# A gated linear attention and a maxout feed-forward block on one core: the written step order, the PSUM rooms and the set of second-engine steps are exchanged for others

## The chip, the cores and the metric

The kernel runs on one core of a Trainium2 chip. The metric is the device time of one execution in microseconds; the time of a kernel is the median of several executions. Five engines of the core work side by side, each on its own list of instructions: TensorE (PE, with its weight loads shown as PEld), VectorE (DVE), ScalarE (ACT), GpSimd (POOL) and SyncE (SP). The last two mainly issue transfers here. Every matmul and every DMA has float32 data; the weights come in memory as 64-bit floats.

## The reference

The attention part keeps, per head, a complex state that each step multiplies by a gate and to which it adds the outer product of k and v; the output is q times the state's real part. The feed-forward part takes the largest of three projections and projects it down.

```python
mag = np.sqrt(a_re * a_re + a_im * a_im)
scale = np.minimum(mag, 0.999) / (mag + 1e-06)
a_re_n, a_im_n = (a_re * scale, a_im * scale)
...
for t in range(S):
    ar, ai = (a_re_n[:, :, t, :, None], a_im_n[:, :, t, :, None])
    new_re = ar * S_re - ai * S_im
    new_im = ar * S_im + ai * S_re
    kv = np.einsum('bhd,bhe->bhde', k[:, :, t], v[:, :, t])
    S_re, S_im = (new_re + kv, new_im)
    y[:, :, t] = np.einsum('bhd,bhde->bhe', q[:, :, t], S_re)
...
h = np.maximum(np.maximum(x @ w1, x @ w2), x @ w3)
return (h @ w_out).astype(np.float32)
```

Here q, k, v, a_re and a_im are 4 batches × 8 heads × 768 tokens × 48; x is 3072 × 384, w1 to w3 are 384 × 768 and w_out is 768 × 384.

## The kernel before, in words

The 3072 tokens are worked in 12 groups, g = 0 to 11. A group is one chunk of 128 tokens of two batches, which the names tell apart by an x or a y. Two batches run through their six chunks, then the other two.

Nothing is left to a scheduler. The string SCHEDULE (line 21) lists 1903 words, each a step and the group that it is for (`dky:0` is step dk of the second sequence of group 0), and `program` (998) runs them in this order through `run` (954). The class Bound (199) ties each engine's instructions to the one before it on that engine, so the string is the order on every engine, and also the order in which SP and POOL issue DMAs. Steps on different engines wait for one another only where data or a buffer demand it. A DMA that waits on SP holds up all DMAs behind it in SP's list.

Every output of TensorE goes to one of four PSUM rooms. `banks` (218) takes the next digit of the string SLOTS (124) as the room. So a step on TensorE waits until the steps that read the room's last contents are done.

The set OTHER (131) names the words that run on their second engine. `copy` (239) is on ScalarE, or on VectorE if the word is in the set; `magnitude` (246) likewise; `increase` (253) is an accumulating DMA issued by POOL, or an addition on VectorE; the loads of q, k and v (379, 385) are issued by SP, or by POOL if in the set. ScalarE needs a table load whenever the next function is of another set, exponential and logarithm on the one side, sine and arctangent on the other (`activation`, 227).

The steps that matter here, by their words:

- Loads: Lr, Li are a_re and a_im of a group (192 KB, tiles ar and ai), Lq, Lk, Lv are q, k, v in four DMAs of 48 KB each (tiles q, k, vb). WL0 to WL11 (`weight_load`, 414) bring a third of a weight matrix each as raw 64-bit words, 768 KB, always on SP, into a borrowed buffer: xhx, strassen or a part of another weight's place (dictionary ROOMS, 138). WL4 and WL7 both use strassen, WL2, WL5 and WL8 use xhx, so a load waits for the last conversion step of the one before.
- Conversion of the raw words to float32 (`weight_step`, 429): Wa on ScalarE, Wb, Wc, We, Wf on VectorE; Wf is the last that reads the raw words. Wg adds w1's negative to w2 or w3, by `increase`: a 384 KB accumulating DMA `w<-w` unless in OTHER.
- Gates of a group (names in line 499): sqr, sqi, add, lnL, expw, expe, lne, relu, Lnop, abs, addw, lnw, half, expL, mulai, mulw, stt, atan, xor, turn. They turn ar and ai into a log magnitude Ln and an angle w; `turn` is the angle's last step. In group 0 they run in two halves, named by 0 and 1.
- cs: TensorE's running sum of the angles; t and nf reduce it to one turn, af, sa and sb make cosine and sine. sums, En, Ek, Eq: running sums of Ln and their exponentials. F, f0 to f3: a few cut-off factors.
- mk, mq, uk, uq: k and q times exponentials and sines, on VectorE. tpk, tpq: transposes on TensorE; Kc, Qc: their copies; Q1, Q2, KB, QB, QG: further scaled copies.
- A, B: score matmuls (64 and 32 small ones). g0 to g3, b0, b1: masks and copies into atm. dk, h0 to h3: state update. y: the output, 128 × 384; x: its copy to SBUF (xT in group 0, part of xhx later).
- T, t, M, m: the product w1·w_out, needed because the kernel takes the maximum over x(w2−w1), x(w3−w1) and 0, and brings w1's part in behind it as x(w1·w_out).
- U, u: up-projection and maximum (U01, U11 and so on: half and weight; group 0 in thirds with x or y, as `U01x:0`). S, P, r, O, o: down-projection, from group 1 on by seven products. D: store. J: joins of weights for the seven products. Cd: four tiny accumulating DMAs of POOL that carry the angle to the next chunk. CL, Z: constants and zeros.

In the order before, VectorE's neighbourhood of the change reads uqy:0, turn:1, mky:0, Wf4:0; SP's reads Lqx:1, WL5, WL7, WL8, Lix:4; TensorE's reads M2:0, csx:1, tpky:0, Fx:1, csy:1, Ay:0, U01x:0, dky:0, U11x:0. Every instruction is recorded through one helper, so all profile rows carry line 208 and are told apart by tile names.

Of the kernel before, what the change touches and what calls it, by code (L numbers as in the profile page):

```python
# [21 lines left out]
Liy:0 sqi1:0 Zg:0 Zf:0 Lry:0 sqr1:0 Lix:0 add1:0 lnL1:0 sqi0:0 Lrx:0 sqr0:0 add0:0 expw1:0 WL0:0 WL3:0 expe1:0 relu1:0  # L22
lne1:0 lnL0:0 xor0:0 Wa0:0 expe0:0 expw0:0 Lnop1:0 xor1:0 abs1:0 lne0:0 half1:0 Wb0:0 Wc0:0 We0:0 Fy:0 pw1:0 f0y:0
relu0:0 WL6:0 Lqx:0 Lnop0:0 Wa3:0 abs0:0 WL10:0 WL9:0 Lix:1 Wf0:0 lnw1:0 sumsx:0 Wa6:0 Wb3:0 half0:0 Wc3:0 Lkx:0 Eqx:0
Wb6:0 f1y:0 expL1:0 We3:0 mulw1:0 pw0:0 Ekx:0 Lrx:1 Liy:1 f3y:0 Wc6:0 lnw0:0 Wf3:0 Lry:1 Fx:0 mulai1:0 expL0:0 mulw0:0
mulai0:0 stt1:0 stt0:0 Enx:0 We6:0 f3x:0 atan0:0 turn0:0 T0:0 atan1:0 t0:0 mkx:0 Wa9:0 Wf6:0 csx:0 turn1:0 Wb9:0 tx:0
mqx:0 Wa10:0 nfx:0 WL11:0 afx:0 csy:0 Wb10:0 ty:0 sqr:1 Wc9:0 Wc10:0 T2:0 nfy:0 sbx:0 sax:0 We9:0 ukx:0 Wf9:0 f1x:0
t2:0 f2x:0 We10:0 Lix:2 uqx:0 Lky:0 f2y:0 tpkx:0 kEnx:0 Wf10:0 f0x:0 sqi:1 Wa11:0 WL1:0 Wb11:0 add:1 sumsy:0 Eky:0
tpqx:0 CL:0 Qcx:0 Kcx:0 Wa1:0 Q2x:0 lnL:1 WL2:0 Q1x:0 Eqy:0 relu:1 Wb1:0 Wc11:0 T1:0 expe:1 Eny:0 Wc1:0 expw:1 abs:1
Lvx:0 Lry:2 t1:0 We11:0 dkx:0 h1x:0 xor:1 Ax:0 Wf11:0 Wa2:0 Lqy:0 lne:1 g0x:0 We1:0 Liy:2 g1x:0 Lkx:1 Wb2:0 QBx:0  # L30
# [7 lines left out]
u02x:0 atan:2 U12y:0 turn:2 sbx:1 Wf7:0 u01y:0 u02y:0 Lix:4 u11y:0 Fy:1 Wg7:0 sumsy:1 Wa8:0 Wb8:0 mkx:1 u12y:0 mqx:1  # L38
U21y:0 sby:1 f0y:1 Wc8:0 csx:2 Lnop:2 f1y:1 f3y:1 Lkx:2 f2y:1 Z4:0 Eky:1 csy:2 Eny:1 u21y:0 Eqy:1 uqx:1 ty:2 tpqx:1
Qcx:1 U21x:0 We8:0 ukx:1 tpkx:1 u21x:0 Lvx:2 Wf8:0 nfy:2 Kcx:1 tx:2 Z3:0 Wg8:0 Lky:1 kEnx:1 sumsx:2 nfx:2 Fx:2 U22y:0  # L40
h0x:1 u22y:0 Lvx:1 QBx:1 say:1 Lqy:2 dkx:1 Liy:3 mqy:1 Q1x:1 Enx:2 Q2x:1 mky:1 afx:2 sax:2 Lvy:2 KBx:1 h1x:1 sbx:2
# [5 lines left out]
lne:3 QBx:2 kEnx:2 lnw:3 Lry:4 U11:1 h3y:1 g1x:2 Cdy:2 g2x:2 u11:1 uqy:2 expL:3 mulai:3 U12:1 g3x:2 u12:1 tpqy:2 Qcy:2
tpky:2 dkx:2 Fy:2 Lnop:3 mulw:3 U01:1 f0y:2 Lqy:3 stt:3 h0x:2 h1x:2 h2x:2 J1:0 f3y:2 sqi:4 Kcy:2 U02:1 f2y:2 sqr:4
h3x:2 atan:3 Lix:5 f1y:2 add:4 Liy:5 J2:0 KBx:2 u01:1 Cdx:2 turn:3 Bx:2 kEny:2 b1x:2 b0x:2 csx:3 tx:3 csy:3 lnL:4
h0y:2 ty:3 KBy:2 u02:1 Fx:3 expe:4 f2x:3 nfx:3 S1:1 nfy:3 f3x:3 S3:1 dky:2 sumsx:3 Q1y:2 h1y:2 Q2y:2 f1x:3 Ekx:3 f0x:3  # L50
Lkx:3 Enx:3 afy:3 QBy:2 Lky:4 h2y:2 S2:1 P1:1 P5:1 S4:1 yx:2 Eqx:3 J4:0 Ay:2 g0y:2 Lrx:5 xx:2 mkx:3 relu:4 Py:1 afx:3
P4:1 h3y:2 expw:4 r1:1 abs:4 addw:4 g1y:2 g2y:2 lne:4 P6:1 xor:4 sax:3 QGy:2 g3y:2 Px:1 sby:3 P7:1 sbx:3 Dx:0 P3:1
mqx:3 r6:1 half:4 h0x:3 P2:1 By:2 r5:1 r7:1 r57:1 oy:1 lnw:4 sumsy:3 b1y:2 b0y:2 Fy:3 ukx:3 Cdx:3 Eny:3 uqx:3 Eky:3
expL:4 ox:1 Cdy:3 Eqy:3 f3y:3 Lvy:3 f0y:3 yy:2 xy:2 tpqx:3 mulai:4 tpkx:3 Qcx:3 mqy:3 Lnop:4 mulw:4 QBx:3 Q1x:3 Lky:3
say:3 stt:4 sqi:5 uqy:3 Lry:5 sqr:5 Kcx:3 KBx:3 mky:3 U01:2 Lvx:3 Q2x:3 U02:2 f2y:3 uky:3 add:5 f1y:3 Dx:1 u01:2 u02:2
tpqy:3 Lqx:4 tpky:3 atan:4 Kcy:3 Ax:3 lnL:5 S3:2 Qcy:3 Liy:6 Bx:3 g0x:3 g1x:3 g2x:3 kEnx:3 Lkx:4 U11:2 turn:4 g3x:3
xor:5 csy:4 QGx:3 Lqy:4 b0x:3 u11:2 b1x:3 csx:4 ty:4 tx:4 nfx:4 afx:4 nfy:4 Q2y:3 dkx:3 sumsy:4 Eqy:4 sumsx:4 Ekx:4
mkx:4 h1x:3 mqy:4 expe:5 kEny:3 Eqx:4 Q1y:3 KBy:3 U12:2 Eky:4 h2x:3 Enx:4 yx:3 expw:5 Eny:4 Ay:3 u12:2 sax:4 P7:2
sbx:4 h3x:3 S1:2 Lry:6 QBy:3 g0y:3 g1y:3 S2:2 P1:2 sby:4 mqx:4 Fx:4 h0y:3 relu:5 Dy:1 xx:3 g2y:3 g3y:3 dky:3 abs:5
Fy:4 QGy:3 h1y:3 h2y:3 h3y:3 r1:2 afy:4 say:4 f0y:4 uqx:4 f2y:4 f3y:4 P5:2 addw:5 P6:2 Py:2 lnw:5 expL:5 uqy:4 ukx:4  # L60
r6:2 f2x:4 lne:5 Lnop:5 Lrx:6 f1y:4 Px:2 S4:2 P2:2 r5:2 P4:2 By:3 h0y:4 Lqx:5 half:5 Cdy:4 f3x:4 r7:2 b0y:3 Lkx:5
Cdx:4 r57:2 mulai:5 f0x:4 mky:4 uky:4 b1y:3 P3:2 ox:2 oy:2 f1x:4 mulw:5 stt:5 yy:3 xy:3 tpqy:4 Qcy:4 Q2y:4 atan:5
turn:5 tpqx:4 Qcx:4 QBx:4 Q1x:4 Q2x:4 Lix:7 tpky:4 Q1y:4 tpkx:4 Lix:6 sqr:6 sqi:6 U11:3 U12:3 u11:3 Kcy:4 add:6 kEnx:4
Kcx:4 csy:5 u12:3 lnL:6 csx:5 expe:6 kEny:4 Ax:4 ty:5 nfy:5 lne:6 xor:6 Ay:4 tx:5 nfx:5 relu:6 expw:6 g0x:4 abs:6 Dy:2
Lvx:4 g1x:4 g2x:4 g3x:4 U01:3 g0y:4 g1y:4 afx:5 Lqy:5 sax:5 g2y:4 u01:3 g3y:4 sbx:5 S3:3 U02:3 h0x:4 KBx:4 QGx:4 dkx:4
u02:3 sumsx:5 half:6 Lvy:4 addw:6 afy:5 lnw:6 expL:6 h1x:4 Lnop:6 h2x:4 h3x:4 S1:3 Dx:2 sumsy:5 dky:4 Lrx:7 Lky:5
Liy:7 Eqx:5 Eqy:5 Eny:5 P1:3 sby:5 mqx:5 h1y:4 P7:3 Eky:5 S2:3 mqy:5 P5:3 Bx:4 Lry:7 mulai:6 b0x:4 P6:3 mky:5 h2y:4
uqx:5 KBy:4 b1x:4 QBy:4 h3y:4 mulw:6 Enx:5 S4:3 yx:4 Ekx:5 sqr:7 By:4 r1:3 r6:3 xx:4 stt:6 Fx:5 r5:3 r7:3 Lvx:5 QGy:4
mkx:5 r57:3 b0y:4 f3x:5 say:5 atan:6 Py:3 Px:3 P3:3 P2:3 turn:6 f0x:5 b1y:4 uqy:5 P4:3 sqi:7 Lqy:6 f2x:5 f1x:5 csx:6
ukx:5 tx:6 csy:6 ty:6 ox:3 yy:4 oy:3 nfy:6 uky:5 xy:4 tpqx:5 nfx:6 Dx:3 sby:6 tpkx:5 add:7 Lvy:5 Qcx:5 Q1x:5 kEnx:5  # L70
Q2x:5 Kcx:5 tpky:5 tpqy:5 Kcy:5 U11:4 u11:4 Fy:5 kEny:5 dkx:5 sbx:6 Qcy:5 Lvy:6 afy:6 xor:7 lnL:7 Lvx:6 f2y:5 f3y:5
f1y:5 h0x:5 f0y:5 Q2y:5 h1x:5 sumsy:6 Lry:8 expw:7 afx:6 Ax:5 g0x:5 Eny:6 relu:7 g1x:5 g2x:5 expe:7 h0y:5 Lky:6 Liy:8
Eqy:6 Q1y:5 abs:7 U01:4 u01:4 sax:6 QGx:5 half:7 Cdx:6 mqy:6 g3x:5 U12:4 say:6 Eky:6 KBx:5 QBx:5 addw:7 lnw:7 mky:6
U02:4 Lrx:8 expL:7 u12:4 Bx:5 uqy:6 Ay:5 b1x:5 mulai:7 lne:7 u02:4 S3:4 Lqx:7 sumsx:6 g0y:5 dky:5 b0x:5 h1y:5 KBy:5
P1:4 P7:4 Enx:6 g1y:5 Eqx:6 Lqx:6 yx:5 QBy:5 Ekx:6 g2y:5 g3y:5 By:5 xx:5 S1:4 mqx:6 tpqy:6 uqx:6 mulw:7 tpqx:6 b0y:5
Dy:3 Qcy:6 P5:4 S2:4 P6:4 b1y:5 stt:7 Px:4 P2:4 Py:4 P4:4 Lnop:7 QGy:5 Lix:8 S4:4 atan:7 r1:4 r6:4 r5:4 r7:4 sqr:8
# [965 lines left out]
```

## Time and profile before

| what | value |
|---|---|
| time, median of 3 runs | 568.42 us (568.22 to 568.48) |
| the profiled execution's own time | 566.42 us |
| its span, from the first to the last instruction | 564.7 us |
| mean granted TensorE clock | 0.978 |
| bytes moved | 47.53 MB, mean 84 GB/s |
| of these HBM | read 33.03 MB, written 4.72 MB |

The profiled execution is 2.0 us below the median of the runs, and 1.7 us lie outside its span. Times in the rows are in microseconds from the span's start. Where the page divides the span into 40 equal slices of 14.1 us, the busy tenths of two engines and the granted clock are:

```
PE   2568799999998999999999999999999999999997
DVE  7999959999998999999999889999998868997324
PEclk9779989999999999999999999999999999999999
```

Each digit is one slice. TensorE is filled from the sixth slice on, and the granted clock is below full speed in a few slices of the first hundred microseconds only. A busy share is an average over such stages, so each stage is looked at by itself.

### The profile page before, as it was taken

What the parts mean: (1) busy time and instruction counts of PE and PEld (TensorE: products, weight loads), DVE (VectorE), ACT (ScalarE), POOL (GpSimd) and SP (SyncE); (2) the same over time, 40 slices, a digit from 0 to 9 for tenths busy, and PEclk for the clock granted to TensorE, in tenths of its full rate; (3) what the DMA queues carried; (4) which work ended last, traced back from release to release, by engine and by line L of the source; (5) the groups of instructions that cost most, each with busy time, mean ns of one, the idle gap of its engine ahead of it and who ended that gap; (6) DMA issues with size and microseconds to landing.
All of it is one profiled execution on the core that took longest, in us unless ns stands there. A gap on an engine that the chain in (4) does not pass through costs nothing.

```text
span 564.7 us, 22778 instructions
## 1 busy us (share of the span) xinstructions
PE 527.8 (93%) x10086; PEld 452.2 (80%) x10086; DVE 490.0 (87%) x777; ACT 391.5 (69%) x668; POOL 153.5 (27%) x243
## 2 busy tenths in 40 slices
PE   2568799999998999999999999999999999999997
...
DVE  7999959999998999999999889999998868997324
...
PEclk9779989999999999999999999999999999999999
...
GB/s 249 267 253 88 193 171 68 104 33 81 78 47 89 53 87 87 141 35 139 59 11 156 58 42 68 99 46 110 76 90 28 30 60 73 3 30 2 2 29 28
DMA packets 108916, 47.53 MB, mean 84 GB/s; under 512 B 95633, under 2 KB 100241, under 8 KB 108817
## 3 DMA queue, kind: packets, MB, share of 16 engines
...
q8 instruction: 79, 1.29, 0.9%
...
HBM read 33.03 MB, written 4.72 MB: 67 GB/s over the span
## 4 chain that ended last, share of the span: by engine, by line
PE 75%; ACT 6%; DVE 2%; issue 1%; SPq 1%; DMA 1%; DVEq 0%; ACTq 0%
PE up L208 30%; PE op L208 21%; PE y L208 6%; PE A L208 4%; PE tp L208 4%; PE dk L208 3%; PE sums L208 2%; PE cs L208 2%; ACT L208 2%; PE F L208 1%; PE B L208 1%; SPq L208 1%; DMA ar<-in_a_re_dram 1%; DVE atm L208 1%; ACT f L208 1%
## 5 line engine op out<-in xcount | busy, mean ns | idle before, releaser
L208 PE MATMUL up<-xhx,w 128*128 128x256 f32 x792 | 177.7, 382 | 0.7 <-ACT K L208 0.4
L208 PEld LDWEIGHTS up<-xhx,w 128*128 128x128 f32 x792 | 148.4, 190 | 22.5 <-ACT K L208 0.6
L208 ACT ACT_TABLE_LOAD x59 | 75.7, 1283 | 1.7 <-PEq L1026 0.8
L208 POOL DMA_DIRECT2D ar<-nf x40 | 35.7, 1261 | 73.9 <-DVE ar L208 71.1
L208 PE MATMUL op<-wo,xhx 128*128 128x192 f32 (+1 forms) x220 | 49.1, 363 | 0.1
L208 DVE TENSOR_TENSOR Q<-Q,f 112x1024 f32<-112x1024 f32 (+1 forms) x48 | 44.8, 951 | 0.7 <-ACT Q L208 0.7
L208 POOL DMA_DIRECT2D k<-in_k_dram x52 | 36.7, 1021 | 30.1 <-DVE uk L208 29.6
L208 DVE TENSOR_TENSOR ot<-ot,op 128x192 f32<-128x192 f32 (+1 forms) x66 | 27.2, 417 | 19.0 <-PE op L208 11.5
L208 POOL DMA_DIRECT2D w<-L x7 | 6.2, 884 | 130.9 <-ACT L L208 65.4
L208 POOL DMA_DIRECT2D vb<-in_v_dram x48 | 34.1, 967 | 27.5 <-PE y L208 27.5
L208 ACT ACTIVATE f<-F 48x232 f32<-48x232 f32 x96 | 34.2, 359 | 10.5 <-PE F L208 8.4
L208 PEld LDWEIGHTS op<-wo,xhx 128*128 128x128 f32 x220 | 36.7, 190 | 4.3 <-issue 0.6
L208 ACT COPY atm<-B 32x128 f32<-32x128 f32 x96 | 24.6, 256 | 21.9 <-DVE atm L208 14.2
L208 PE MATMUL y<-atm,vb 128*32 128x64 f32 x1152 | 38.5, 221 | 0.7 <-POOL uk L208 0.5
L208 PE MATMUL y<-QG,g 112*32 112x64 f32 x1408 | 37.5, 219 | 0.0
L208 PEld LDWEIGHTS y<-atm,vb 128*32 128x32 f32 x1152 | 31.9, 109 | 6.7 <-issue 2.9
L208 PEld LDWEIGHTS y<-QG,g 112*32 112x32 f32 x1408 | 34.5, 109 | 0.0
L208 PE MATMUL op<-wo,strassen 128*128 128x192 f32 x176 | 33.0, 331 | 0.0
L208 PE MATMUL A<-Q,K 112*32 112x80 f32 x1536 | 31.5, 234 | 1.4 <-issue 1.3
L208 PE MATMUL op<-w,strassen 128*128 128x192 f32 x176 | 32.3, 328 | 0.0
L208 DVE COPY_PREDICATED atm<-masko,A 128x256 f32<-128x256 uint8 x72 | 30.8, 433 | 1.4
L208 ACT COPY ot<-op 128x192 f32<-128x192 f32 (+1 forms) x13 | 4.4, 342 | 38.0 <-PE op L208 37.9
...
## 6 DMA issues: line engine op xcount, KB each, us to landing
...
```

What stands on the lines that cost most here:

```text
L208: ins = f(*a, **kw)
```

## The change

Only three module-level strings change; no function does. SCHEDULE keeps the same 1903 words in another order (it is printed in one line more, so the helper's line 208 is 209 after). SLOTS has the same number of digits, other rooms. OTHER has 73 words for 72: Kcx:2, Kcy:11, Lnop:7, Lnop:9, abs:7, addw:5, addw:11, afx:8, afx:11, afy:3, 5, 9 and 10, u01:8, u01:9, xx:7 and xy:11 go to VectorE; Kcy:9, Kcy:10, Qcy:8, abs:3, 9 and 11, addw:3, addw:7, Lnop:4, afx:4, 5 and 6, afy:11, u11:11, xx:10, xy:5, 6 and 10 go from it; and among the q, k and v loads Lky:0 moves to POOL early while Lqy:0, Lkx:1, Lqy:1 and Lky:1 move to SP.

As it falls on the engines around 50 to 70 us: VectorE gets uqy:0, We4:0, Wf4:0, mky:0, turn:1; SP gets Lkx:1, Lrx:2, Lqy:0, WL5, Lqx:1, Lqy:1, Lix:4, WL7, WL8; TensorE gets M2:0, csy:1, tpky:0, csx:1, Ay:0, dky:0, U01x:0, Fx:1. ScalarE has 53 table loads for 59, SP 228 DMA issues for 236, POOL 204 for 197. TensorE's instructions are the same ones.

```diff
SCHEDULE = """
...
-half:1 g2x:0 Wc2:0 g3x:0 pw:1 Wf1:0 M0:0 afy:0 lnw:1 h2x:0 WL4:0 Lnop:1 expL:1 We2:0 Wa4:0 KBx:0 mulai:1 mulw:1 h3x:0
-Cdy:0 Wb4:0 Bx:0 stt:1 Lrx:2 sqr:2 Wf2:0 say:0 sby:0 QGx:0 M1:0 b1x:0 atan:1 mqy:0 Wc4:0 uqy:0 Wg1:0 b0x:0 yx:0 Cdx:0
-tpqy:0 sqi:2 add:2 xor:2 turn:1 lnL:2 Lvy:0 relu:2 Lqx:1 WL5:0 We4:0 xx:0 Qcy:0 mky:0 M2:0 Wf4:0 expe:2 Wa5:0 csx:1
-uky:0 m0:0 m1:0 Q2y:0 Lqy:1 tpky:0 Fx:1 tx:1 Kcy:0 f0x:1 Q1y:0 nfx:1 csy:1 QBy:0 Ay:0 expw:2 Wg2:0 abs:2 kEny:0 Wg4:0
-Wb5:0 WL7:0 U01x:0 ty:1 g0y:0 f1x:1 lne:2 nfy:1 dky:0 g1y:0 f2x:1 f3x:1 addw:2 Wa7:0 half:2 Cdx:1 u01x:0 U11x:0 Z2:0
-g2y:0 Wc5:0 g3y:0 KBy:0 h1y:0 By:0 b1y:0 b0y:0 QGy:0 lnw:2 Cdy:1 We5:0 Wb7:0 Wf5:0 sumsx:1 h2y:0 u11x:0 expL:2 mulai:2
-yy:0 xy:0 mulw:2 Eqx:1 Wc7:0 Ekx:1 Enx:1 U02x:0 h3y:0 afx:1 sax:1 stt:2 Wg5:0 afy:1 We7:0 U02y:0 U01y:0 U11y:0 WL8:0
...
-h2x:1 Ekx:2 Eqx:2 uqy:1 afy:2 Oy:0 oy:0 Liy:4 tpqy:1 h3x:1 uky:1 QGx:1 Bx:1 Qcy:1 Ax:1 tpky:1 f1x:2 f0x:2 f2x:2 f3x:2
-Q1y:1 Kcy:1 Lqx:2 g0x:1 Q2y:1 sby:2 say:2 U22x:0 g1x:1 g2x:1 g3x:1 mkx:2 Lrx:3 u22x:0 Lix:3 KBy:1 Lvy:1 sqi:3 b1x:1
-Ay:1 sumsy:2 kEny:1 mqx:2 Lky:2 QBy:1 uqx:2 b0x:1 Eky:2 U12x:0 u12x:0 Eqy:2 yx:1 xx:1 ukx:2 Lry:3 tpqx:2 tpkx:2 Eny:2
...
+Ax:0 Wb1:0 g0x:0 Wf11:0 g1x:0 expe:1 Wc1:0 WL2:0 g2x:0 We1:0 relu:1 xor:1 Wf1:0 WL4:0 abs:1 half:1 dkx:0 h1x:0 pw:1
+Liy:2 Wa2:0 Eny:0 g3x:0 Wb2:0 h2x:0 Wc2:0 lne:1 Lnop:1 h3x:0 Lvy:0 We2:0 lnw:1 expL:1 Lkx:1 M0:0 Wg1:0 afy:0 Wa4:0
+sby:0 Bx:0 mulw:1 QGx:0 Wf2:0 Lrx:2 mulai:1 sqr:2 Lqy:0 sqi:2 say:0 Wb4:0 mqy:0 b1x:0 Wc4:0 Cdx:0 M1:0 stt:1 uqy:0
+We4:0 WL5:0 Cdy:0 Lqx:1 b0x:0 add:2 atan:1 yx:0 lnL:2 Z2:0 tpqy:0 relu:2 Lqy:1 Wf4:0 Qcy:0 mky:0 Lix:4 xx:0 expe:2
+Wg2:0 turn:1 uky:0 Wa5:0 M2:0 csy:1 m1:0 tpky:0 Kcy:0 Q1y:0 csx:1 Q2y:0 Wg4:0 xor:2 m0:0 Ay:0 tx:1 kEny:0 dky:0 Wb5:0
+expw:2 abs:2 lne:2 QBy:0 h1y:0 g0y:0 nfx:1 g1y:0 g2y:0 g3y:0 U01x:0 WL7:0 Wc5:0 half:2 ty:1 addw:2 u01x:0 KBy:0 Wa7:0
+Fx:1 nfy:1 Cdy:1 f1x:1 f0x:1 f3x:1 f2x:1 We5:0 sumsx:1 Cdx:1 QGy:0 Enx:1 By:0 b1y:0 b0y:0 lnw:2 U02x:0 Wf5:0 Ekx:1
+expL:2 Eqx:1 Wb7:0 u02x:0 afx:1 h2y:0 Wc7:0 yy:0 xy:0 sbx:1 U11x:0 WL8:0 Wg5:0 mulw:2 Lnop:2 u11x:0 Wa8:0 mulai:2
...
+sumsx:2 nfy:2 h0x:1 Enx:2 tx:2 u22y:0 Lvx:1 mqy:1 Ekx:2 dkx:1 say:1 Lky:1 nfx:2 h1x:1 QBx:1 Lix:3 Oy:0 Lkx:2 sbx:2
+afx:2 h2x:1 mky:1 h3x:1 uqy:1 tpqy:1 uky:1 Fx:2 Eqx:2 oy:0 Qcy:1 Q1x:1 KBx:1 tpky:1 QGx:1 f0x:2 Kcy:1 Ax:1 mkx:2 Q1y:1
+Q2y:1 Lry:3 g0x:1 Lvy:1 g1x:1 g2x:1 Bx:1 f1x:2 afy:2 f3x:2 U22x:0 u22x:0 say:2 sby:2 g3x:1 Ay:1 b0x:1 sax:2 KBy:1
...
 SLOTS = """
-0123123232301023123030312302103010321320130202301021023203131032132120312031230123130120310312032102
-3010312030313210323102310231033213021321031203121302131201023103210213012321302103101313031203120210
-2310203103201320230132013123012312023120210312320131201300210230130123120312012032013021303212301303
-2212
+0123132323131013201311303203013130132312301202132031201120320312101320123102132103131201321230123013
+2013120130001203210230213201311201320120312301203210230211023202310320132120312130103101230312031201
+3201320102301231210231203213201210201301203102130210230132330132013202310230130213021023013020312131
+2323
 """
 OTHER = set("""
-abs1:0 Lqy:0 Lkx:0 Lvx:0 Lkx:1 Lvy:0 Lqy:1 Lky:1 Wg7:0 Wg8:0 Lkx:2 Lqx:2 Lvy:2 Lky:2 abs:3 addw:3 Lvx:3 Lqy:3 afx:3
-abs:4 Lnop:4 afx:4 Kcx:4 afx:5 Kcx:5 xy:4 Lkx:6 u11:4 Lqx:6 Lvx:6 Lvy:6 afx:6 addw:7 xy:5 Lkx:7 Kcy:6 Lqy:7 Lky:7 xx:6
-afy:7 abs:8 xy:6 Lqy:8 Qcy:7 afy:8 Lvy:8 abs:9 addw:9 Qcx:8 Lkx:9 u01:7 Lqy:9 Qcy:8 Lvy:9 Lkx:10 Lky:9 Lvx:10 Kcy:9
-Lvy:10 abs:11 Lky:10 Kcy:10 Lvx:11 xx:10 Lqy:11 afy:11 Lky:11 Lvy:11 xy:10 Qcy:11 u11:11 u01:11
+abs1:0 Lkx:0 Lvx:0 Lky:0 Lvy:0 Lvx:1 Wg7:0 Wg8:0 Lqy:2 Lqx:2 Lvy:2 Kcx:2 Lqx:3 Lvy:3 Lky:3 Lqy:3 afx:3 abs:4 afy:3
+Lvx:4 Lqy:4 Kcx:4 Lky:4 Lvy:5 addw:5 Lqx:5 Lky:5 afy:5 Kcx:5 xy:4 Lkx:6 u11:4 Lqy:6 Lvx:6 Lvy:6 Lnop:7 abs:7 Lkx:7
+Kcy:6 Lky:7 xx:6 afy:7 abs:8 Lqx:8 Lvx:8 Qcy:7 Lky:8 xx:7 afx:8 afy:8 Lvy:8 Lnop:9 addw:9 Qcx:8 Lqx:9 Lkx:9 u01:7
+Lvx:9 afy:9 Lvx:10 u01:8 Lvy:10 afy:10 Lkx:11 addw:11 u01:9 Lqy:11 Lky:11 afx:11 Kcy:11 Qcy:11 xy:11 u01:11
 """.split())
```

More of the change, by code (lines that the diff above doesn't have):

```diff
@@ L21 @@
 SCHEDULE = """
[L22 to L30, printed above, removed]
-half:1 g2x:0 Wc2:0 g3x:0 pw:1 Wf1:0 M0:0 afy:0 lnw:1 h2x:0 WL4:0 Lnop:1 expL:1 We2:0 Wa4:0 KBx:0 mulai:1 mulw:1 h3x:0
@@ L37 @@
-yy:0 xy:0 mulw:2 Eqx:1 Wc7:0 Ekx:1 Enx:1 U02x:0 h3y:0 afx:1 sax:1 stt:2 Wg5:0 afy:1 We7:0 U02y:0 U01y:0 U11y:0 WL8:0
[L38 to L41, printed above, removed]
@@ L47 @@
[L47 to L51, printed above, removed]
@@ L52 @@
[L52 to L76, printed above, removed]
@@ L107 @@
-P1:8 mqy:10 b1y:9 P6:8 Px:8 KBx:10 addw:11 P3:8 xor:11 yy:9 half:11 r1:8 r6:8 Py:8 lnw:11 expL:11 lne:11 xy:9 P4:8
-P2:8 Cdy:10 Lky:10 S3:8 QBx:10 r5:8 ox:8 P7:8 h0x:10 xx:9 r7:8 Fy:10 r57:8 f3y:10 f1y:10 Cdx:10 uqy:10 f0y:10 dkx:10
-f2y:10 U11:9 h1x:10 mulw:11 mulai:11 Q2x:10 U01:9 h2x:10 h3x:10 tpqy:10 mky:10 stt:11 atan:11 uky:10 oy:8 Dy:8 turn:11
-tpky:10 Lqy:11 u01:9 u11:9 csx:11 tx:11 csy:11 Kcy:10 nfx:11 ty:11 nfy:11 Ax:10 g0x:10 g1x:10 afy:11 Qcy:10 Bx:10
-Lnop:11 kEny:10 U12:9 Lvx:11 g2x:10 g3x:10 U02:9 afx:11 h0y:10 u12:9 S3:9 b0x:10 QGx:10 Q2y:10 sumsy:11 u02:9 S1:9
@@ new lines @@
+half:3 u11:1 Lry:4 g3x:2 h0x:2 tpqy:2 Cdx:2 Qcy:2 tpky:2 Cdy:2 dkx:2 sqr:4 Fy:2 f0y:2 Liy:4 sqi:4 QBx:2 u12:1 h1x:2
+U02:1 Liy:5 J3:0 h2x:2 J1:0 f1y:2 h3x:2 KBx:2 U01:1 J2:0 S3:1 Kcy:2 kEny:2 Dx:0 turn:3 add:4 Lky:4 Lix:5 f3y:2 f2y:2
+u01:1 Bx:2 Q1y:2 csx:3 tx:3 csy:3 ty:3 h0y:2 u02:1 b0x:2 nfx:3 sumsx:3 Enx:3 afx:3 nfy:3 Lry:5 b1x:2 dky:2 Ekx:3 QBy:2
+Fx:3 P1:1 S1:1 S2:1 J4:0 lnL:4 Lrx:5 f3x:3 P5:1 h1y:2 Eqx:3 expe:4 yx:2 f2x:3 expw:4 h2y:2 Q2y:2 f0x:3 KBy:2 f1x:3
+xx:2 xor:4 Ay:2 P7:1 g0y:2 g1y:2 relu:4 S4:1 abs:4 lne:4 addw:4 P6:1 half:4 sbx:3 Lkx:3 mkx:3 Lvx:3 r1:1 Py:1 Px:1
@@ new lines @@
+Cdx:3 sby:3 r6:1 r5:1 Lnop:4 mqx:3 sax:3 h0x:3 P4:1 g2y:2 g3y:2 r7:1 lnw:4 P2:1 h3y:2 P3:1 By:2 sumsy:3 expL:4 b0y:2
+r57:1 Fy:3 b1y:2 QGy:2 Eny:3 Lvy:3 ox:1 ukx:3 Eqy:3 uqx:3 f0y:3 yy:2 Eky:3 oy:1 sqr:5 Lky:3 xy:2 mulai:4 tpkx:3 tpqx:3
+Qcx:3 mulw:4 stt:4 Q2x:3 Kcx:3 atan:4 afy:3 say:3 Liy:6 Q1x:3 QBx:3 f2y:3 mqy:3 mky:3 uky:3 uqy:3 f3y:3 U01:2 QGx:3
+f1y:3 U02:2 Lkx:4 Cdy:3 tpqy:3 KBx:3 u01:2 u02:2 Qcy:3 Q1y:3 Lvx:4 tpky:3 Ax:3 sqi:5 Kcy:3 turn:4 add:5 Bx:3 S3:2
+g0x:3 g1x:3 g2x:3 Lqy:4 g3x:3 U11:2 kEnx:3 u11:2 csx:4 tx:4 Dx:1 csy:4 Lqx:4 b1x:3 b0x:3 dkx:3 Lry:6 ty:4 xor:5 nfx:4
```

122 lines of the change are left out of this document (80 added, 42 removed).

## The prediction

> **What bounds the kernel now.** I read first the busy totals on the page, then busy time by stretch (columns: stretch, its length, then busy us and count for PE, PEld, DVE, ACT, POOL, the granted clock, the DMA share, GB/s).
>
> ```profile
> span 564.7 us, 22778 instructions
> PE 527.8 (93%) x10086; PEld 452.2 (80%) x10086; DVE 490.0 (87%) x777; ACT 391.5 (69%) x668; POOL 153.5 (27%) x243
> ...
> q8 instruction: 79, 1.29, 0.9%
> ```
>
> ```profile
> 10.00:65.70 55.70, 42.32 (x598) 27.16 (x593) 54.97 (x86) 50.47 (x82) 28.27 (x44) 0.85 0.90 207
> 0.00:65.70 65.70, 42.56 (x598) 27.43 (x599) 61.41 (x106) 57.66 (x97) 36.15 (x75) 0.87 0.89 210
> 65.70:69.75 4.05, 0.00 (x0) 0.04 (x1) 4.05 (x10) 3.63 (x7) 2.43 (x4) 0.86 1.14 226
> 69.75:75.43 5.68, 5.63 (x81) 5.31 (x81) 3.13 (x5) 0.86 (x2) 5.39 (x9) 0.50 0.38 87
> 75.43:80.00 4.57, 4.10 (x142) 3.51 (x142) 0.18 (x2) 2.98 (x8) 2.98 (x6) 1.00 1.16 240
> 0.00:80.00 80.00, 52.29 (x819) 36.28 (x820) 68.78 (x120) 65.13 (x113) 46.94 (x89) 0.85 0.88 204
> 80.00:115.00 35.00, 33.03 (x627) 27.01 (x630) 33.21 (x51) 32.90 (x57) 9.83 (x16) 1.00 0.51 97
> 115.00:561.00 446.00, 442.42 (x8658) 388.90 (x8646) 387.42 (x607) 293.46 (x500) 96.76 (x138) 1.00 0.31 62
> ```
>
> TensorE is idle for 564.7 − 527.8 = 36.9 us. Of these 80 − 52.29 = 27.7 lie before 80 us, 2.0 between 80 and 115, 3.6 between 115 and 561, and 3.6 in the tail. From 115 us on TensorE is the bound (442.42 of 446), and the change leaves its work as it is, so a reordering there can return 3.6 us at the very most. From 10 to 65.7 VectorE is the bound (54.97 of 55.70). Between the two is the one hole that neither explains: 65.7 to 69.75, where TensorE runs nothing, and after which its clock is granted at 0.50.
>
> What ends that hole? The timeline (start, length, engine, instruction; in brackets idle time before it and who ended it):
>
> ```profile
> 65.55 0.19 PEld L208 LDWEIGHTS up<-xT,w 128*128 128x128 f32 x1
> 69.80 0.59 PE L208 MATMUL up<-xT,w 128*128 128x128 f32 x2 [4.18 <-DVE KB L208]
> 69.80 0.51 PEld L208 LDWEIGHTS up<-xT,w 128*128 128x128 f32 x2 [4.07 <-issue]
> ```
>
> The matmul stands waiting with its weights loaded at 65.74, and the releaser named, VectorE's KB, belongs to something older; the weight load beside it says "issue". So the sequencer had no instruction to issue. The instruction queue has 79 packets and 1.29 MB: 16.3 KB a packet, and 2 × 10086 TensorE instructions over 79 are 255 a packet. TensorE's program comes in blocks of about 256. Up to 65.70 it has issued 598 + 599 rows and some waits without a row, close to 1217, the start of a block if each has 256 and the first ends near 193. The DMA view by stretch shows that block late (queue: packets, MB, busy share):
>
> ```profile
> DMA packets 856, 1.24 MB, mean 213 GB/s; under 512 B 32, under 2 KB 472, under 8 KB 856
> q0 software_dynamic: 456, 0.45, 55.9%
> q1 hardware_dynamic: 400, 0.79, 50.7%
> ...
> q0 software_dynamic: 212, 0.23, 119.2%
> q8 instruction: 1, 0.02, 5.1%
> ```
>
> The first three rows are 61.6 to 67.4 us: no instruction packet, while a 768 KB weight load (q1) and an accumulating copy (q0) ran. The last two are 67.4 to 68.6: q1 is gone, there the block comes, and TensorE restarts 1.2 us after.
>
> **The change part by part.** It permutes the step list, hands out the four PSUM rooms in another order, and exchanges some steps and loads between engines. TensorE's work is the same. Four terms.
>
> *The late block.* These rows are the big transfers and VectorE's steps around them:
>
> ```profile
> 52.80 0.97 DVE L208 SCALAR_TENSOR_TENSOR w<-xhx 128x768 int32<-128x768 int32 x1
> 55.20 0.97 DVE L208 TENSOR_TENSOR uq<-CS,q 128x768 f32<-128x768 f32 x1
> 57.81 0.97 DVE L208 SCALAR_TENSOR_TENSOR w<-w,ar 128x768 f32<-128x768 f32 x1
> 60.02 0.97 DVE L208 SCALAR_TENSOR_TENSOR w<-strassen,xhx 128x768 int32<-128x768 int32 x1
> ```
>
> ```profile
> 37.13 3.48 SPq L208 DMA_DIRECT2D q<-in_q_dram  x4
> 53.83 0.37 SPq L208 DMA_DIRECT2D xhx<-in_moe_w_dram  x1
> 61.06 0.37 SPq L208 DMA_DIRECT2D strassen<-in_moe_w_dram  x1
> 72.93 0.48 SPq L208 DMA_DIRECT2D ai<-in_a_im_dram  x1
> 56.47 2.45 POOL L208 DMA_DIRECT2D q<-in_q_dram  x4 [3.09 <-DVE uq L208]
> 58.90 1.34 POOL L208 DMA_DIRECT2D w<-w  x1
> 61.29 1.27 POOL L208 DMA_DIRECT2D w<-w  x1 [1.04 <-DVE w L208]
> 61.62 0.87 PE L208 MATMUL cs<-w,upto 128*64 128x192 f32 x8
> ```
>
> Before: step Wf4 ends at 60.02 + 0.97 = 60.99, the weight load WL7 that overwrites its raw data is issued at 61.06, and the preceding TensorE block (with csx:1) starts at 61.62. If the next block is asked for about then, it stands behind WL7 and behind the copy of 61.29. After: Wf4 is moved ahead of mky:0, turn:1 and xor:2 on VectorE (at most 0.97 each, together about 2.5, an estimate), to end near 58.5. But on SP WL7 now stands behind WL5, two q loads of four issues each, and an a_im load that came after WL8. The second q load was on POOL; it waits for the step uqy:0, over at 55.20 + 0.97 = 56.17. Four issues take 3.48 and the a_im load 0.48, so WL7 goes at 56.17 + 3.48 + 0.48 = 60.1, its bytes on q1 behind those of nine other issues. POOL, rid of 2.45 us of q issues, brings its copies forward by up to that. On TensorE csy:1 now starts that preceding block, some 0.6 earlier (≈61.0), and the late block now begins in dky:0 instead of at an `up`. The margins are below 1 us, so that the request comes ahead of the weight bytes is a choice: I take it because the copy on q0, which lasted until the block came, is earlier by 2.4 and q1's weight bytes later in their queue. Worth 4.07 to 4.18 us, and 0 if not.
>
> The Trainium skill, page DMA: Bandwidth & Descriptors, section Queues, rings and completion order, speaks against this: each DMA engine takes turns between its queue rows, a packet at a time. By that rule a block would never wait for a whole transfer, and moving the transfer would return nothing; the 61.6 to 67.4 rows rather show a wait as long as the transfers, and what that rule would give stands as rival A.
>
> *The half clock behind it.* From 69.75 to 75.43 5.63 us are busy at 0.50; at full clock this is 2.8. It follows the idle hole, so it goes with it: −2.8, or 0 with the hole.
>
> What is late next is VectorE. It idles 69.75 to 80 for 10.25 − 3.13 − 0.18 = 6.9 us, so up to 6.9 of the 7.0 can move forward on it; but its own chain is full until 65.7 and up to 69.75 (4.05 of 4.05), so some TensorE steps will wait for it. +1.0 taken (0 to +4, the 4 being the row before: the hole merely renamed a wait for VectorE).
>
> *Tables.* The order has 53 table loads for 59:
>
> ```profile
> L208 ACT ACT_TABLE_LOAD x59 | 75.7, 1283 | 1.7 <-PEq L1026 0.8
> ```
>
> Six at 1.283 us are 7.7 us of ScalarE. ScalarE is 69% busy and where TensorE is the bound this hides behind it (293.46 of 446); only from 80 to 115, with ScalarE at 32.90 of 35, it can matter, and TensorE idles 2.0 us there. Taken −0.5 (−2.0 to 0).
>
> *Moves between engines and rooms.* Seventeen small steps come to VectorE and eighteen leave it for ScalarE or POOL, which nearly balances in its 490 us. These and the rest of the reordering lie after 115 us, beneath TensorE. There I bound it by idle already there, −1.5 (less than half of 3.6), and on the other side by fetch gaps of this kind of row:
>
> ```profile
> 402.54 0.23 PE L208 MATMUL A<-Q,K 112*32 112x80 f32 x1 [0.87 <-issue]
> 107.20 0.53 PE L208 MATMUL A<-Q,K 112*32 112x80 f32 x17 [0.46 <-issue]
> ```
>
> A block of small matmuls is over fast, and the next one is not there yet. By my count of the steps in each 256 instructions, blocks of under 3.3 us of work rise from four to eight. Four new ones at 0.46 to 0.87 are +1.8 to +3.5, offset by some idle removed: +1.0 taken (−1.5 to +6, the 6 with a clock drop behind one).
>
> *Sum,* against the profiled execution's own 566.42 (the span and 1.7 around it): −4.2 − 2.8 + 1.0 − 0.5 + 1.0 = −5.5, that is 560.9. The median of the runs shown is 568.42, 2.0 above the profiled execution, so 562.9, rounded to **563.0**. Its own range is 560.5 (no VectorE loss, −1.5 for the rest) to 566.
>
> **The rivals.**
>
> *A. The change doesn't do what it says: the block is as late as before.* For it: the margins above, under 1 us either way; and a block that came late with nothing in its way:
>
> ```profile
> 0.00:98.15 98.15, 69.50 (x1107) 51.55 (x1109) 86.20 (x146) 81.74 (x143) 51.85 (x97) 0.88 0.82 185
> DMA packets 142, 0.12 MB, mean 18 GB/s; under 512 B 109, under 2 KB 109, under 8 KB 141
> q8 instruction: 1, 0.02, 5.3%
> ```
>
> The second row is 98.15 to 104.7: a block after 2216 rows, at 18 GB/s, not fetched for 6.5 us; the third is 104.7 to 105.8, where it comes. So a fetch can be late because it was asked late. Then the hole and its half clock remain and the time is 568.4 − 0.5 + 1.0 ≈ 568.9. Against it: the packet comes in the very 1.2 us from which q1 is gone, and a request as late as the one at 104.7 should fall there by chance only. This is also where the rule of the skill named above would lead, since the transfers would then not be the cause.
>
> *B. The hole moves to the block with Ax:1 and gets worse: slower.* In the new order the block at tpqy:1, Fx:2, tpky:1, Ax:1 holds only small matmuls, some 3 us, where before it held Oy:0 too:
>
> ```profile
> 62.43 0.66 PE L208 MATMUL tp<-ident,uk 64*112 64x64 f32 x16
> 63.02 0.56 PE L208 MATMUL F<-cuts,Ln 64*48 64x29 f32 x32
> 64.31 1.31 PE L208 MATMUL A<-Q,K 112*32 112x80 f32 x64
> ```
>
> (Two tp at 0.66 or less, F at 0.56, A at 1.31: 3.2 at most.) If its successor's packet is as late as the one of 98.15 to 104.7, 6.55 us, and restart follows 1.2 to 2 us behind, TensorE stands 6.55 + 2.2 − 3.2 ≈ 5.6, and runs as after 69.75 with half a clock, 2.8 more. It decides from where the block's work falls below the lateness of the fetch, 6.55. With the first hole gone: 563 + 8.4 = 571.4. For it: the late fetch at a low DMA load. Against: TensorE felt only 0.46 us of it then (at 107.20), because the work in between was long, and the 3.6 us idle from 115 to 561, over some 68 blocks, speak for fetches that are mostly in time.
>
> The skill's page Runtime: NRT & Kernel Launch, section Instruction fetch mechanics, says that crossing a block's boundary is mostly hidden; by it B falls away. The 4.18 us above is the counter-example.
>
> **How the numbers follow.** Forecast 0.52, A 0.22, B 0.26. Within 0.2% (1.14 us, about what a measurement of this kernel tells from no change) lies half of A, 0.11, and 0.01 of the forecast's tail; A's other half goes to slower (0.05) and faster (0.06). Faster 0.57, same 0.12, slower 0.31. The range goes from 559 (tables and rest at their good ends) to 573 (B with a loss at another thin block).
>
> **What would show it.** Right: no gap over 1 us at TensorE's first block after dky:0 begins; an instruction packet before WL7's bytes; the granted clock at 1.00 from 65 to 76; VectorE idle under 2 us from 66 to 80; 53 table loads; busy TensorE from 115 to 561 within 1 us of 442. A: the same 4 us gap near 65 with the packet after the transfers. B: a gap of several us, and half a clock after it, around Ax:1 of group 1. The forecast is wrong too if VectorE is named as releaser of a new gap between 60 and 80.

## The result, and the profile after

| | old order | new order | ratio, 95% interval |
|---|---|---|---|
| first comparison, 8 runs each | 568.38 us | 564.99 us | 0.9935 (0.9912 to 0.9958) |
| again, in a later round, 29 and 12 runs | 566.33 us | 564.64 us | 0.9978 (0.9955 to 1.0001) |

The change makes the kernel faster, by 3.4 us in the first comparison and 1.7 in the second; the second interval just reaches 1, and a gain of 2.4 us (0.9957) lies in both. Single runs of either kernel spread over 3 to 7 us. The two profiled executions hide the gain: the old one (566.42) was 2.0 below its median, the new one (566.65) 1.7 above its own. So I took a second profile of the new kernel, 564.59 us.

The page of the new kernel, span, busy totals and the table loads:

```profile
span 564.9 us, 22784 instructions
...
PE 526.3 (93%) x10086; PEld 450.5 (80%) x10086; DVE 491.1 (87%) x776; ACT 384.6 (68%) x664; POOL 160.4 (28%) x250
...
L209 ACT ACT_TABLE_LOAD x53 | 68.0, 1283 | 1.6 <-PEq L1027 0.8
```

Busy time by stretch of the new kernel (columns as before):

```profile
0.00:80.00 80.00, 51.48 (x826) 35.37 (x826) 71.75 (x123) 67.16 (x116) 43.76 (x80) 0.89 0.86 204
80.00:115.00 35.00, 32.89 (x680) 27.48 (x682) 34.56 (x55) 30.64 (x56) 10.86 (x18) 1.00 0.50 96
115.00:561.00 446.00, 441.59 (x8588) 387.62 (x8582) 384.22 (x599) 286.75 (x494) 105.77 (x153) 1.00 0.31 61
66.00:80.00 14.00, 10.97 (x280) 9.48 (x268) 11.09 (x21) 10.46 (x23) 9.12 (x12) 0.88 0.68 160
```

Up to 115 us TensorE has done 826 + 680 rows of matmuls for 819 + 627 before; behind that nothing got better. At the disputed border of two instruction blocks, first the old kernel's row behind its hole, then the new kernel's timeline:

```profile
69.80 2.72 PE L208 MATMUL up<-xT,w 128*128 128x128 f32 x12 [4.18 <-DVE KB L208]
...
66.26 0.78 PE L209 MATMUL dk<-vb,uk 64*64 64x48 f32 x34
68.95 0.87 PE L209 MATMUL dk<-vb,uk 64*48 64x48 f32 x30 [1.91 <-issue]
69.75 2.93 PE L209 MATMUL up<-xT,w 128*128 128x128 f32 x12
...
75.47 1.60 PE L209 MATMUL up<-xT,w 128*128 128x128 f32 x12 [1.05 <-ACT f L209]
```

and the same place in its second profile:

```profile
65.47 0.78 PE L209 MATMUL dk<-vb,uk 64*64 64x48 f32 x34
66.71 0.67 PE L209 MATMUL dk<-vb,uk 64*48 64x48 f32 x30 [0.47 <-issue]
67.60 1.58 PE L209 MATMUL up<-xT,w 128*128 128x128 f32 x12 [0.23 <-PE dk L209]
...
73.33 1.43 PE L209 MATMUL up<-xT,w 128*128 128x128 f32 x8 [0.65 <-issue]
```

The border lies within dky:0, as counted beforehand: 34 pairs run, then TensorE waits on nothing but issue. The hole of 4.18 us has become 1.91 and 0.47. Where 1.91 is left, the twelve `up` matmuls behind it still take 2.93 us, about as long as after the old hole (2.72); behind the short gap they take 1.58. The second profile stops once more one block later (0.65), which the old kernel does not.

When did the packet come? DMA in the slices 62.5 to 66.3 (first three rows) and 66.3 to 67.5 of the new kernel's first profile, and its transfers as SP and POOL issue them:

```profile
DMA packets 1645, 0.88 MB, mean 232 GB/s; under 512 B 1144, under 2 KB 1492, under 8 KB 1645
q0 software_dynamic: 364, 0.36, 66.9%
q1 hardware_dynamic: 1281, 0.53, 50.5%
...
q1 hardware_dynamic: 217, 0.42, 93.3%
q8 instruction: 1, 0.02, 5.8%
```

```profile
61.08 0.60 SPq L209 DMA_DIRECT2D ai<-in_a_im_dram  x1
61.80 0.72 SPq L209 DMA_DIRECT2D strassen<-in_moe_w_dram  x1
...
60.02 1.23 POOL L209 DMA_DIRECT2D w<-w  x1 [2.56 <-DVE w L209]
```

It came at 66.4, in the middle of the weight load and not ahead of it; what had just ended was POOL's queue q0. In the old kernel it was the other way round: q1 had ended and q0 still ran. The second profile differs: there the packet came at 64.5, with nearly all of the load still to come. The trace lets one count this, since the load is 384 packets of 2048 bytes: 384 of them went ahead of the block's packet in the old kernel, 170 in the new one's first profile and 18 in its second.

### The profile page after: what moved, and what is told of

Same layout as the page of the kernel before. It is cut to its first block, busy times and chain, and to the rows that moved or that the text cites. A ratio compares the mean times of both kernels' runs of the same rounds, so it can differ in the third digit from the quotient of the medians.

```text
span 564.9 us, 22784 instructions
## 1 busy us (share of the span) xinstructions
PE 526.3 (93%) x10086; PEld 450.5 (80%) x10086; DVE 491.1 (87%) x776; ACT 384.6 (68%) x664; POOL 160.4 (28%) x250
## 4 chain that ended last, share of the span: by engine, by line
PE 76%; ACT 11%; DVE 7%; issue 3%; DMA 2%; SPq 0%; DVEq 0%; ACTq 0%; POOLq 0%
PE up L209 32%; PE op L209 20%; PE y L209 5%; PE A L209 4%; PE dk L209 3%; PE tp L209 3%; PE cs L209 3%; DVE xhx L209 2%; PE sums L209 2%; ACT f L209 2%; ACT L209 1%; PE B L209 1%; PE F L209 1%; ACT L L209 1%; ACT atm L209 1%
## 5 line engine op out<-in xcount | busy, mean ns | idle before, releaser
L209 POOL DMA_DIRECT2D k<-in_k_dram x48 | 31.9, 771 | 80.3 <-DVE uk L209 66.9
L209 POOL DMA_DIRECT2D ar<-nf x40 | 37.6, 1403 | 36.8 <-DVE ar L209 27.5
L209 POOL DMA_DIRECT2D vb<-in_v_dram x56 | 41.2, 1044 | 20.0 <-PE y L209 18.3
L209 POOL DMA_DIRECT2D Ln<-e x9 | 12.7, 1408 | 78.6 <-ACT e L209 59.6
L209 DVE TENSOR_TENSOR xhx<-xhx,up 128x768 f32<-128x768 f32 x22 | 20.9, 951 | 15.5 <-PE up L209 15.2
L209 POOL DMA_DIRECT2D q<-in_q_dram x40 | 26.6, 805 | 23.3 <-DVE uq L209 23.3
```

The lines of the kernel that those rows point to most:

```text
L209: ins = f(*a, **kw)
```

## Experiments

**The new kernel once more,** unchanged:

> The new kernel as it is, for a second profile of it. If the two profiled executions that came out alike in time (566.4 old, 566.7 new) were chance, this one lies near 565.0 or below, with 0.4 to 2 us at the border in dky:0 and the difference to the first profile within the first 80 us.

Measured: 564.64, its profiled execution 564.59, the gap 0.47; the difference to the first profile is there by 80 us (the table of rows below). That the first two profiles were equally long was chance.

**Which part of the order.** Five kernels are mixtures: the words of one order up to a seam, then the remaining words in the other order, each with its own engines (the lines below say it in words and are not the kernels' text). Each experiment is compared by its ratio to the old kernel in the same round, whose median was 566.59 us for the `start` and shifted kernels, 566.33 for the other three mixtures and 568.14 for the rest. The PSUM rooms of one part are renamed where needed; in the mirror image `start_after` three rooms at its seam are chosen anew.

```diff
-SCHEDULE = old
+start_before: old[:440] + new rest;  start_after: new[:440] + old rest
+region_new: old[:180] + new[:305] + old rest;  region_old: new[:180] + old[:305] + new rest
+old_to_930: old[:930] + new rest
```

> The first 440 steps (to about 115 us) in the old order with their old rooms and engines, the rest in the new order. Theory 1, the gain of 3.4 us (568.4 to 565.0) is made at the start: the time is that of the kernel before, 568.4, within 0.8. Theory 2, it is made in the rest (53 table loads, fewer waits of TensorE after 115 us): 565.0 within 0.8.

> The mirror image: the first 440 steps new, the rest old (three PSUM rooms just behind the seam are chosen anew). Theory 1: 565.0 within 0.8. Theory 2: 568.4 within 0.8. If both halves matter, both mixed kernels lie between, near 566.7.

Measured: `start_after` 564.42, ratio 0.9950 (0.9926 to 0.9975), as theory 1 says. `start_before` took 577.09, 1.0193 (1.0166 to 1.0220), outside of both theories. Of its waits between 110 and 126 us, this one is new:

```profile
PE B L208 <- DVE K L208: 7.6, 1, 7.6
```

The old start reaches its work of group 1 later than the new rest expects it: a wait of 7.6 us at the seam, of a kind that neither order has. It says nothing on the question, so I moved the seam to a place where the two orders differ in two words only.

> The first 930 steps (to about 230 us) old, the rest new; at this seam only two words differ. Theory: all of the gain is ahead of it, ratio 1.000 within 0.003. Rival, the rest of the reordering and its fewer table loads give something: 0.997 or less.

Measured: 568.44, 1.0034 (1.0012 to 1.0056), just above the theory's limit. With the old start there is no gain, and the hole is there, in the timeline:

```profile
70.43 2.72 PE L208 MATMUL up<-xT,w 128*128 128x128 f32 x12 [4.55 <-DVE KB L208]
```

> The old kernel, but with the steps from about 50 to 77 us (words 180 to 305) in the new order, on the new engines and in the new rooms; everything ahead and behind is old. Theory, the gain sits in this stretch (the late block and the slow clock behind it): ratio to the kernel before 0.9935 within 0.003, a gap of at most 2 us at the border in dky:0. Rival, the gain comes from the first 50 us or from 77 to 115: ratio 1.000 within 0.003.

> The mirror image: the new kernel with words 180 to 305 in the old order. Theory: the gap of about 4 us at the border in front of U01x:0 comes back and the ratio to the kernel before is 1.000 within 0.003. Rival: 0.9935 within 0.003 with the gap there or not.

Measured: `region_new` 565.07, 0.9990 (0.9970 to 1.0011); `region_old` 570.64, 1.0075 (1.0048 to 1.0102). The first fits the rival by its time, the second neither. But in this round the whole change gave no more than 0.9978, and `region_new` with 565.07 is not clear of the new kernel's 564.64, so its time decides little. In `region_new` the gap at the border was 2.06 us, just above the expected limit. In `region_old` the gap came back with 3.13 us, but two seam waits of 2.74 (at 53 us) and 2.53 (at 92) stand beside it. The share of the stretch can't be read from this pair, since the seams bring waits of their own.

A count that needs no mixture: the time at which TensorE starts its n-th row (matmuls, weight loads and those waits that have a row, in order of start, counted from 0), by profile, in us:

```
profile        row 961   1217   3265   end    end - row 3265
old               61.7   69.8  120.3  564.7  444.4  (rest old)
old_to_930        61.9   70.4  120.4  567.3  446.9  (rest new)
new               62.6   68.9  118.8  564.9  446.1  (rest new)
new, again        61.8   66.7  116.4  562.9  446.5  (rest new)
start_after       62.0   67.6  116.2  561.8  445.6  (rest old)
region_new        61.5   68.5  118.0  563.1  445.1  (rest old)
```

Up to row 961 the orders are level. From there to row 1217, the block in front of the border and its gap, the old start needs 8.1 and 8.5 us, the new one 4.9 to 6.3 (7.0 in `region_new`). To row 3265 the new start is 1.5 to 4 us ahead, and the new rest then gives back about 1.5 (446.5 against 445.0 on average; the two rests do not hold quite the same matmuls, TensorE being busy 436.7 to 438.0 us in them). What is left is of the size of the measured gain.

**Is it the block?** The old and the new kernel with 16 small matmuls ahead, 64 instructions of TensorE:

```diff
+    scrap = psum.tile([P, 2, 512], FP, tag="ps0", name="scrap")
+    for _ in range(16):
+        mm(out=scrap[0:NF, 0, 0:NF], lhsT=cuts[0:L64], rhs=cuts[0:L64], start=True, stop=True)
     program(SCHEDULE, 0)
```

> The old kernel with 16 small matmuls (64 TensorE instructions, into a PSUM room that nobody reads) ahead of everything, where TensorE is idle for 9.8 us anyway. Orders, transfers and rooms are the old ones; only the borders between blocks of 256 instructions move 64 instructions forward. Theory, the block was asked for behind the large transfers: the border goes from U01x:0 into Ay:0 and the block is asked for near M2:0 (57.5 us) instead of at csx:1 (61.6), so it comes before the transfers, the hole of 4.2 us and the half clock behind it (2.8) are gone, about 562.4. Rival, TensorE waits there for something else than its instructions: the hole stays in front of U01x:0, 568.4. Second rival, a block comes late whatever the transfers do: the hole moves into Ay:0 and the time stays at 568.4.

> The new kernel with the same 64 instructions ahead. In its profile a gap of 1.9 us is left within dky:0, ended by nothing but issue, and behind it the clock is 0.73 for 5 us. Theory: with the border 64 instructions earlier the block is asked for near 58 us and the gap and its slow clock go: 1.9 + 1.2, about 562. Rival, the gap comes from the transfers' load as such and moves with the border: 565.0.

Measured: 575.18, 1.0156 (1.0122 to 1.0190), and 577.14, 1.0170 (1.0142 to 1.0198). The times fit nothing expected, but the place of the hole does. The timeline of the old kernel so shifted, and its DMA from 58 to 61 us:

```profile
67.12 1.31 PE L208 MATMUL A<-Q,K 112*32 112x80 f32 x64
68.37 1.60 PE L208 MATMUL up<-xT,w 128*128 128x128 f32 x12
...
q8 instruction: 1, 0.02, 3.1%
```

No hole in front of U01x:0, none in Ay:0, and `up` at full speed. The block was asked for at 59.6, came at 60.6, and the weight load went out at 62.2. So the hole was TensorE's instructions, which came late when asked for at 61.7 and in time when asked for at 59.6. Matmul by matmul the shifted kernel is 2.8 us behind the old one at number 480, ahead of the hole, and 3.5 in front of it at number 800: in this stretch the hole and what follows it had cost 6.3. The time went elsewhere, seen in the same kernel's timeline and in TensorE's groups from 115 us on:

```profile
285.16 0.88 PE L208 MATMUL tp<-ident,uq 64*112 64x64 f32 x24
287.42 0.44 PE L208 MATMUL tp<-ident,uq 64*112 64x64 f32 x8 [1.37 <-issue]
...
L208 PE MATMUL A<-Q,K 112*32 112x80 f32 x1280 | 26.9, 234 | 3.2 <-issue 3.2
```

Twelve borders behind 110 us now stop TensorE for 0.3 to 1.5 us each, 10.4 in all (before, three behind 100 us with 1.6 in all): the new borders cut off blocks that hold little but small matmuls. From matmul 1600 (1.4 us in front) to the last (8.9 behind) the shifted kernel loses 10.3 us, so these stops account for the loss. In both shifted profiles, behind 80 us, of the 22 blocks with under 3.0 us of work 18 were followed by a gap above 0.2 us, of 21 with 3.0 to 4.5 nine, and of 101 longer ones none. In the unshifted orders only 6 blocks of three profiles (the old kernel's and the new one's two) are under 3.0, three of them with a gap.

**Which transfer holds the block?**

```diff
 OTHER = set("""
-abs1:0 Lqy:0 ...
+abs1:0 Wg4:0 Lqy:0 ...
```

(and the same word in the new kernel's set), and, for the weight load's place on SP:

```diff
-... Lqy:1 Wf4:0 Qcy:0 ... g3y:0 U01x:0 WL7:0 Wc5:0 ...
+... Wf4:0 WL7:0 Lqy:1 Qcy:0 ... g3y:0 U01x:0 Wc5:0 ...
```

> The old kernel with one word added to OTHER: Wg4:0 is an addition on VectorE (0.97 us) and no longer a 384 KB accumulating DMA of POOL. It was issued at 61.29, and the late block's packet came at 67.5. Theory a, the accumulating copies of POOL's queue hold up the block: the packet comes near 63.5 (the copy of 58.90 is through by then) and the hole of 4.2 us shrinks below 1; with its slow clock and 1 us more of VectorE the time falls by 4 to 6. Theory b, the 768 KB weight load holds it up: the packet comes near 67 again, when that load is through, and the time stays within 1 us or rises by 1.

> The new kernel with the same word added. Its own packet came at 66.4, in the slice in which POOL's queue fell silent while the weight load still ran, with a gap of 1.9 us. Theory a: packet near 63, gap gone, 1.9 + 1.2 of slow clock less, 1 more on VectorE: about 2 us below the new kernel, 563. Theory b: nothing changes but VectorE's 1 us, 565 to 566.

> The new kernel with the weight load WL7 directly behind Wf4 on SP, ahead of the second q load and the a_im load (issued near 59.8 for 61.8). By the prediction's reason, the load's bytes then stand ahead of the block asked for at 62.6: the gap grows from 1.9 toward 4 and the time to 567 to 569. By theory a of POOL's queue: the gap stays at 1 to 2.5 and the time at 565 within 1.

Measured: 566.09, 0.9974 (0.9948 to 1.0001); 566.33, 0.9967 (0.9947 to 0.9987); 565.28, 0.9949 (0.9924 to 0.9974). The rows at the border, old kernel without the copy, new kernel without it, new kernel with the early weight load:

```profile
68.87 1.50 PE L208 MATMUL up<-xT,w 128*128 128x128 f32 x12 [2.65 <-DVE nf L208]
```

```profile
69.56 0.61 PE L209 MATMUL dk<-vb,uk 64*48 64x48 f32 x29 [0.39 <-issue]
```

```profile
68.30 0.67 PE L209 MATMUL dk<-vb,uk 64*48 64x48 f32 x30 [0.54 <-issue]
```

Without the copy the old hole shrank from 4.2 to 2.65, between the theories; the packet came at 66.4, as the last bytes of the weight load went. The early weight load, issued at 58.96 and so 4 us ahead of the request, did no harm at all: 376 of its 384 packets were through when the block was asked for. So this run does not test what a load does that is asked for just ahead of the block. In five profiles with the new order the gap was 0.5 to 1.9, in three with the old one 3.7 to 4.6; the packet follows its request by 2.6 to 3.8 us there and by 5.2 to 6.0 in the old order. A count over the profiles, with the request taken as the start of the block before:

```
profile             load's packets     request     gap,
                    ahead, of 384      to packet   us
old                 384                5.8         4.18
old_to_930          384                6.0         4.55
start_before        382                5.2         3.73
region_old          379                4.8         3.13
old without copy    384                4.1         2.65
region_new          376                4.8         2.06
new                 170                3.8         1.91
start_after         102                3.3         1.06
new, six tables      12                2.7         0.69
new, again           18                2.7         0.47
new without copy    302                3.2         0.39
```

The longer the gap, the more of the weight load went ahead of the block, with the last row as the exception. In all of them the load was issued 0.5 to 1.5 us ahead of the request. Its first packet followed the request by 1.5 us in the old kernel and by 2.8 and 2.5 in the new one's two profiles. That the load holds the block up is thus likely, but no run changes this alone, and it is not the only cause: in the new kernel shifted by 64, the packet of the block with this number came 3.0 us after its request with none of the load ahead. The Trainium skill, DMA: Bandwidth & Descriptors, Queues, rings and completion order, lets each engine take turns between queues by packet; that a block's packet comes behind 376 or more of the load's 384 packets in six profiles does not look like that alone.

None of these three is clear of the new kernel, so none is shown to be better. In the new kernel with the early weight load, as in two more of the six profiles with the new start, the next border stops TensorE again (0.65 to 1.01 us): a part of the hole can have moved there.

**Table loads.**

```diff
+RELOAD = set("Eky:1 Ekx:2 lnL:4 sbx:4 expL:5 Eqx:5".split())
 ...
         T["word"] = "%s:%d" % (name, g)
+        if T["word"] in RELOAD:
+            act.preload_act_table_set(T["set"])
```

> The new kernel with six more table loads of 1.283 us, which reload the set that is there: two between 80 and 115 us, one between 115 and 200, three between 200 and 300. The prediction took -0.5 for six fewer (0 to -2.0): 565.5. If ScalarE were on the path behind 115 us it would be up to 5 us more, 570; if all is hidden, 565.0.

Measured: 570.78, 1.0052 (1.0024 to 1.0079); by the new kernel's two ratios this is 6.6 and 4.2 us more than the new kernel, for 7.7 us of loads. From row 3265 to the end it takes 450.6 us for the new kernel's 446.1 and 446.5. One group of TensorE from 115 to 561 us, this kernel first, then the new one:

```profile
L210 PE MATMUL y<-atm,vb 128*32 128x64 f32 x1008 | 35.0, 221 | 2.1 <-ACT atm L210 1.5 <-ACT E L210 0.7
```

```profile
L209 PE MATMUL y<-atm,vb 128*32 128x64 f32 x1008 | 35.0, 221 | 1.0 <-ACT atm L209 1.0
```

ScalarE is busy 64% of that stretch, and yet four loads there cost about 4 us. TensorE's waits for ScalarE behind 115 us rise from 2.6 to 5.3 us, and a block's border at 244.6 us stops it for 1.1 more. The words were picked by place, not for slack, so this is the price of a load that nothing was arranged around.

## Why the prediction was right, and where it was off

The forecast was 563.0; 564.99 and 564.64 were measured. Direction and place of the gain were right, its size too large: 5.5 against 3.4 and 1.7. Of the signs that were named for it, a gap of at most 1 us and a packet ahead of nearly all the weight bytes are there in the second profile and not in the first; the granted clock, 0.88 from 66 to 80 us in both, is not.

- **The late block, −4.2.** That TensorE stood for want of its instructions is shown by the shifted kernels. The term was mis-sized: the gap went from 4.2 to 1.9 and 0.5, so −2.3 to −3.7, and 0.65 came back one border later in the second profile. The choice "the request comes ahead of the weight bytes" did not tell the orders apart: the request did so in the old kernel too (61.7, first weight packet at 63.2), and all 384 packets still went ahead of the block. What changed is how many of them do, 170 and 18. The reason given for the choice fits the rows: POOL's copy was issued at 60.0 and 59.2 for 61.3, and the weight bytes began later behind the request. The margin under 1 us that the prediction named is seen in the spread between the two profiles.
- **The half clock, −2.8.** That it goes with the hole is right for most profiles and not a rule. Behind gaps of 3.7 to 4.6 the twelve `up` matmuls took 2.72 us in all three profiles with the old order, behind gaps of 0.5 to 1.1 they took 1.6 in four with the new one. In the first profile of the new order, with its 1.9, the slow matmuls stayed. Against it stand 1.50 us behind a gap of 2.65 in the old kernel without the copy, and 2.60 behind one of 0.39 in the new kernel without it; and in the second profile of the new kernel the y matmuls run slow from 74.7 to 77.1 (three of them in 0.41 us for 0.24 in the first). What sets the slow matmuls off stays open.
- **VectorE, +1.0.** It idles 14 − 11.09 = 2.9 us between 66 and 80, more than the 2 that were announced, and 1.3 in the second profile. The new waits of TensorE there are mostly for ScalarE, such as 1.05 us for ACT f at 75.5; the second profile has one for VectorE (nf), of 0.30.
- **Tables, −0.5.** Not confirmed. The rest with the fewer loads is not faster than the old rest. The reasoning "ScalarE has idle time, so its loads hide" does not hold for the six added loads. In the old order the 59 loads can have cost little from 115 to 561, where TensorE idles 3.6 us for all reasons together; that its steps are arranged around them is likely, but no run shows it.
- **The rest, +1.0.** The size was about right, the reason wrong. New stops at thin blocks were expected; only one border behind 115 us stops the new kernel in its first profile (1.20, before 0.87), two in its second (1.01 and 0.41). What it lost are mostly small waits for ScalarE, like the 1.0 for ACT atm above. The count of thin blocks used 3.3 us as its limit, and many blocks just below that limit stop nothing.
- **Rival B** did not happen at Ax:1, where neither profile of the new kernel has a gap at a border. Its mechanism exists all the same: shifted by 64 instructions both orders paid for it and ended 1.6 and 1.7% above the old kernel. The rule in Runtime: NRT & Kernel Launch, Instruction fetch mechanics, of the Trainium skill, that crossing a border is mostly hidden, agrees with the old kernel and the new one behind 115 us (stops of 0.9 to 1.4 us in all) and not with the shifted ones.
- **The range.** Without VectorE's loss and with −1.5 for the rest the prediction's own terms give 563.0 − 1.0 − 2.5 = 559.5, not 560.5; the stated 559 covers it.
